# Eight plain steps and 32 doubles in a spectral layer with an MLP: plain steps that read the last 64 features from one tile, and a new plan for the work beside them

## The chip, the cores and the metric

The kernel runs on one core of one Trainium2 chip. A core has a matrix engine (TensorE, in the profile PE, with its weight loads as PEld), VectorE (DVE), ScalarE (ACT), GpSimd (POOL) and SyncE (SP), which issues nearly all DMAs. Each engine works off a queue of its own in order and waits on semaphores for the others. SBUF is the on-chip memory; TensorE writes to PSUM, from where VectorE and ScalarE fetch the results. The metric is device time in microseconds (us).

## The reference

```python
def layernorm(x): ...                                   # over the last axis
X = rfft2(layernorm(x)) * (w_r + 1j * w_i)              # x: 1 x 2048 x 576
h = x + irfft2(X, s=(2048, 576))
h2 = h + relu(layernorm(h) @ w1) @ w2                   # w1: 576 x 4608, w2: 4608 x 576
```

Everything is fp32. A matmul of the MLP is written as three products of rounded parts: each operand is split into a high part (`hi`) and the rest (`lo`), and hi·hi, hi·lo and lo·hi are added up in PSUM.

## The kernel before

**Forward stage** (0 to 31 us). The Fourier transforms are matmuls with fixed tables. The 2048 rows form 16 row tiles; for each tile t VectorE takes the statistics (`stat1`, `aggr1`, `row1`), GpSimd a power (`pow1`, L255), VectorE and GpSimd a sum and a difference (`add1` L263, `sub1` L258), ScalarE scales the table (`scale1`, L267, L268), and `fwd_a(t)` does eight matmuls of 64x128 and four of 64x64 (`rest`) for each half and lets ScalarE move the result out of PSUM. The steps of neighbouring tiles are interleaved by the loop over t.

**Middle and inverse stages** (to about 150 us). Sixteen frequency groups are multiplied by the weights and transformed back. The string `STEPS` sets the order by hand: each word is one call, and a word with "=" is a job that is told of below. `project(t)` (words j) writes the normalized rows, transposed, into the tile `xc[c]` of their chunk of 512 rows (c = 0 to 3): places 0 to 4 hold the hi part of the 576 features, 6 to 9 the lo part, and the 64 rows of the last 64 features stand in place 2. Behind the last `project` of a chunk five DMAs on SyncE (L579, L580), the "spread", copy these rows, 32 at a time, to other rows of places 5 and 2.

**Plain steps.** A step (g, c) applies weight group g (256 of the 4608 hidden features) to chunk c. `mm1(i, a)` makes one half of the hidden tile of step i: 14 matmuls of 128x512, the last two for the last 64 features, of which one reads place 2 and one place 5. When both halves are there, ScalarE takes the hi part out of PSUM (L638) and VectorE the lo part (L639). `mm2(i, q)`, q = 0 to 3, makes one output tile of 128 rows: 12 matmuls of 128x288, and VectorE adds the result to the output (L632). The list `steps` has ten steps, numbered from 0; END is the last. `mm1` of step i + 1 is written ahead of `mm2` of step i. From step 3 on one PSUM bank serves mm1 and three others rotate through mm2 (`ring`); the last output tile of step END − 1 is done in two halves.

**Doubles.** The other weight groups are done for two chunks at a time: `doubles` lists (g, p), and pair p = 0 means chunks 0 and 1, p = 1 chunks 2 and 3. A double is a scheme in the manner of Strassen and Winograd with seven products, each with 7 matmuls of 128x512 (`l1_prod`, L826) and 12 of 128x288 (`second`, L931), VectorE adding the results (L941). `slot(d)` interleaves the first halves of double d + 1 with the second halves of double d, and `slot_last` does the last one, half of it as plain products. `weights(d, r)` spreads the weight work for the next doubles over a slot.

**Work beside the plain steps.** Doubles need sums of the chunks' rows, T1 to T4. They are made in eight groups (0 to 7), each by these jobs: L loads a group (SyncE), S makes the four sums (two on VectorE, L673 and L674, two on GpSimd, L675 and L676), H and I take the hi parts (ScalarE), W and X the lo parts (VectorE, two pairs of L694 and L695 in a job). Results of pair 1, and some of pair 0, pass through buffers (`stage`) and are stored to memory from there, to be loaded again by `load_sum`. The first doubles' weights are summed on GpSimd (`w1_sums`, `w2_sums`) and split into hi (ScalarE) and lo (mostly GpSimd, some VectorE). The list `JOBS` says which job follows which `mm2`, from step 3 on. Queues run in the order in which this is written.

## Time and profile before

| | |
|---|---|
| time, median of 3 runs (lowest, highest) | 965.82 us (965.75, 966.11) |
| the profiled execution's own time | 965.46 us |
| its span | 963.7 us |
| granted TensorE clock, mean | 0.999 |
| first double's first product (L826) | at 258.10 us |
| last matmul of TensorE starts its last group | at 957.28 us |

The span runs from the first to the last instruction of the profile; some 1.8 us of the time lie outside it. A row of the timeline has the start, the length, the engine, the line, the operation, the written and read tiles by name, the shapes and the count. A row of a group has the busy time, the mean length of one in ns, and the idle time before its members with what ended it. TensorE's matmuls overlap in the records, so that the distance of two starts tells more than a length.

### The profile page before, as it was taken

The numbers are of one execution on the slowest core, as the hardware profiler recorded it, in microseconds if no ns is written. First come the engines' busy times: TensorE is split into PE (matmuls) and PEld (weight loads), VectorE is DVE, ScalarE is ACT, GpSimd is POOL, SyncE is SP. The second block draws the span as 40 slices with busy tenths as digits, with TensorE's granted clock in tenths as the row PEclk, the third lists the DMA queues.
The fourth block names the chain that finished last, engine by engine and source line by source line (L and its number), as shares of the span: only waits on it lengthen the run. The fifth ranks groups of instructions, "written<-read, shape, count | busy, mean of one in ns | idle before, by whom it ended". The sixth has DMA issues, their size and how long they took to land.

```text
span 963.7 us, 18094 instructions
## 1 busy us (share of the span) xinstructions
PE 955.7 (99%) x6658; PEld 850.1 (88%) x6658; DVE 770.6 (80%) x1226; ACT 466.7 (48%) x912; POOL 646.1 (67%) x783
## 2 busy tenths in 40 slices
PE   9999999999999999999999999999999999999997
PEld 7777778999988999999999999999999999999997
DVE  8577996687768888887888888888878888878886
ACT  6544558323355454545445444554554545444441
POOL 7213787514788777878686878767787768687842
PEclk9999999999999999999999999999999999999999
DMA  7974727557639264563728091836456372819365
GB/s 205 237 188 111 183 97 261 170 205 256 212 118 326 90 238 145 185 199 129 257 71 302 29 325 45 284 98 231 152 176 207 122 262 66 303 35 318 103 213 154
DMA packets 122840, 176.09 MB, mean 183 GB/s; under 512 B 7552, under 2 KB 102400, under 8 KB 122752
## 3 DMA queue, kind: packets, MB, share of 16 engines
q1 hardware_dynamic: 121584, 173.61, 55.9%
q10 hardware_dynamic: 1168, 1.33, 0.4%
q8 instruction: 53, 0.87, 0.4%
q14 instruction: 35, 0.29, 0.1%
HBM read 150.53 MB, written 23.07 MB: 180 GB/s over the span
## 4 chain that ended last, share of the span: by engine, by line
PE 96%; DVE 1%; DMA 1%; ACT 1%; issue 0%; SPq 0%; POOL 0%
PE h L826 36%; PE d L931 35%; PE d L156 24%; DMA C<-C 1%; PE d L564 1%; PE h L931 0%; DMA X<-in_A_x_dram 0%; DVE st L242 0%; ACT X L159 0%; ACT e L159 0%; ACT C L159 0%; DVE A L941 0%; DVE e L414 0%; DVE e L415 0%; DVE A L937 0%
## 5 line engine op out<-in xcount | busy, mean ns | idle before, releaser
L941 DVE TENSOR_TENSOR A<-A,d 128x576 f32<-128x576 f32 x428 | 317.5, 752 | 84.1 <-PE d L931 71.2
L931 PE MATMUL d<-X,D 128*128 128x288 f32 x1476 | 224.3, 294 | 0.1
L931 PEld LDWEIGHTS d<-X,D 128*128 128x128 f32 x1476 | 211.0, 188 | 10.5 <-DVE A L941 0.3
L826 PE MATMUL h<-B,e 128*128 128x512 f32 x658 | 166.8, 392 | 0.0
L159 ACT ACTIVATE e<-h 128x512 f32<-128x512 f32 x93 | 55.6, 597 | 188.0 <-PE h L826 187.9
L826 PEld LDWEIGHTS h<-B,e 128*128 128x128 f32 x658 | 118.3, 188 | 20.4
L353 POOL TENSOR_TENSOR e<-e,e 128x512 fp32r<-128x512 f32 (+3 forms) x68 | 89.8, 1320 | 57.9 <-ACT e L159 55.3
L642 ACT ACTIVATE e<-e 128x512 f32<-128x512 f32 x93 | 58.8, 633 | 107.5 <-DVE e L884 45.2
L826 PE MATMUL h<-X,e 128*128 128x512 f32 x434 | 110.0, 392 | 0.0
L353 POOL TENSOR_TENSOR X<-e,X 128x576 fp32r<-128x576 f32 (+1 forms) x34 | 49.9, 1469 | 62.8 <-ACT X L159 60.7
L826 PEld LDWEIGHTS h<-X,e 128*128 128x128 f32 x434 | 78.0, 188 | 13.4
L159 ACT ACTIVATE e<-e 128x256 fp32r<-128x256 f32 (+5 forms) x171 | 78.6, 489 | 14.3 <-DVE e L673 6.1
L850 POOL TENSOR_TENSOR A<-e 128x256 f32<-128x256 f32 x61 | 48.0, 787 | 28.4 <-DVE X L840 25.3
L840 DVE TENSOR_TENSOR D<-A,D 128x512 fp32r<-128x512 f32 x61 | 63.3, 1038 | 1.7 <-ACT D L159 1.7
L931 PEld LDWEIGHTS d<-X 128*128 128x128 f32 x372 | 55.6, 188 | 5.3 <-issue 0.4
L931 PE MATMUL d<-X 128*128 128x288 f32 x372 | 58.9, 294 | 0.1
L931 PE MATMUL d<-X,e 128*128 128x288 f32 x360 | 57.1, 294 | 0.0
L826 PE MATMUL h<-F,e 128*128 128x512 f32 x217 | 55.0, 392 | 0.0
L852 POOL TENSOR_TENSOR A<-e,A 128x256 f32<-128x256 f32 x61 | 52.9, 867 | 0.8 <-DVE A L848 0.8
L156 PE MATMUL d<-e,D 128*128 128x288 f32 x384 | 53.3, 295 | 0.0
L826 PE MATMUL h<-C,e 128*128 128x512 f32 x210 | 53.3, 393 | 0.0
L156 PEld LDWEIGHTS d<-e,D 128*128 128x128 f32 x384 | 51.9, 188 | 1.4 <-DVE A L632 0.4
(174 smaller groups left out, 1850.9 us busy)
## 6 DMA issues: line engine op xcount, KB each, us to landing
X<-t0T SPq DMA_DIRECT2D x16, 768.0 KB
X<-t1T SPq DMA_DIRECT2D x16, 768.0 KB
e<-in_B_w_dram SPq DMA_DIRECT2D x18, 576.0 KB
e<-in_B_w_dram SPq DMA_DIRECT2D x18, 512.0 KB
X<-t0T SPq DMA_DIRECT2D x16, 512.0 KB
X<-t1T SPq DMA_DIRECT2D x16, 512.0 KB
B<-t1T SPq DMA_DIRECT2D x8, 768.0 KB
B<-t1B SPq DMA_DIRECT2D x8, 768.0 KB
```

Of the source, the lines that this page charges most:

```text
L156: nc.tensor.matmul(o, l, r, start=start, stop=stop)
L159: nc.scalar.activation(o, i, AF.Copy, **kw)
L353: eng.tensor_sub(l, v, h)
L564: nc.tensor.transpose(pz[:, 128 * ORDER[b]:128 * ORDER[b] + 128], y[:, 128 * b:128 * b + 128], ident)
L642: nc.scalar.activation(o, i, AF.Relu)
L826: nc.tensor.matmul(o, a, b, start=bool(first) and n_ == 0, stop=n_ == len(ops) - 1, skip_group_check=not first)
L840: (eng or nc.vector).tensor_sub(f[1], v, f[0])
L850: nc.gpsimd.tensor_sub(s3, p0[:, :256], p0[:, 256:])
L852: nc.gpsimd.tensor_sub(s4, p1_[:, :256], s2)
L931: nc.tensor.matmul(P[tt], l[:, q], r, start=first and n_ == 0, stop=end and n_ == 2, skip_group_check=whole and not first)
L941: nc.vector.tensor_add(xt, xt, P)
```

## The change

The plain steps (2, 3) and (2, 2) go, and a double (2, 1) comes as the last one, so that the doubles are (2, 0), all pairs of groups 3 to 17, and (2, 1): 32 in place of 31. The weight work of `weights` runs on through the last slots, and the outputs of pair 0 are stored one slot earlier.

In the plain steps both matmuls of the last 64 features read place 2: the weight tile holds the 64 rows twice, in hi (`rest[0]`), and in lo with zeros below (`rest[1]`). So the spread is no longer read by plain steps. It becomes a job: F does the four DMAs to place 5, G the one within place 2. The small lo part of `project` is made on GpSimd (j) or VectorE (J), as the string says.

In the forward stage odd tiles do `rest` first and even tiles last, and the last tile's steps stand within the loop's own turn, its subtraction on VectorE.

`JOBS` has 31 entries, one at each place where `work()` is called: behind each `mm1` and `mm2` of steps 3 to 6, and in the seven turns of the last step. A "d" puts lows (W, X) or a weight split (V) on VectorE, otherwise they are on GpSimd; R runs a part of the weights' preparation, V a split, T a load. V4 is the split of T12, V5 that of T34. `stage` grows from four buffers to six.

```diff
+        elif t % 2:
+            rest(p)
         for h in range(2):
             for k in range(2):
                 for j in range(2):
                     q = slice(64 * j, 64 * j + 64)
                     mm(p[:, 512 * j + 128 * h:512 * j + 128 * h + 128], dims(G[q], (k, 321 - k)[h], [2, 128]),
                        caf[q, 64 * k:64 * k + 128], k == 0, k == 1)
-        if not end:
+        if t % 2 == 0:
             rest(p)
         act(dims(zx, 2 * t, [2048, 5 - end], [32, 64], [1, 2]), dims(p, 0, [64, 5 - end], [1, 64], [512, 2]))
 
...
             sub1(t)
         if t < NT:
             aggr1(t)
-        if old:
+        if 1 <= t < NT:
             scale1(t - 1)
+        if t == NT - 1:
+            row1(t)
+            pow1(t)
+            add1(t)
+            sub1(t, nc.vector)
+            scale1(t)
         if t >= 2:
             fwd_a(t - 2)
 
...
+        if g < FIRST:
+            for k in range(2):
+                nc.sync.dma_start(v4[64 * k:64 * k + 64], w1[512:576, f])
+            return
...
-        for k in range(2):
-            split_rest(rest[k], v4[:, k], nc.gpsimd)
+        act(rest[0], v4)
+        nc.gpsimd.tensor_sub(rest[1][:64], v4[:64], rest[0][:64])
+        nc.gpsimd.tensor_sub(rest[1][64:], rest[0][64:], rest[0][64:])
...
-        made[t // CH] += 1
-        (nc.gpsimd if t < 8 and made[t // CH] < CH else nc.vector).tensor_sub(dst[64:, 2, q], zt[64:, 256:384], dst[64:, 2, q])
-        if made[t // CH] == CH:
-            u = dst.bitcast(F32)
+        eng.tensor_sub(dst[64:, 2, q], zt[64:, 256:384], dst[64:, 2, q])
+
+    def spread(c, half):
+        u = xc[c].bitcast(F32)
+        if half:
             for a, b in ((0, 32), (32, 32), (64, 96), (96, 96)):
                 nc.sync.dma_start(u[a:a + 32, 5], u[b:b + 32, 2])
+        else:
             nc.sync.dma_start(u[32:64, 2], u[0:32, 2])
...
-    steps = [(0, 0), (0, 1), (0, 2), (1, 1), (0, 3), (1, 3), (1, 0), (1, 2), (2, 3), (2, 2)]
-    FIRST = 2
+    steps = [(0, 0), (0, 1), (0, 2), (1, 1), (0, 3), (1, 3), (1, 0), (1, 2)]
...
-        ops += [(rest[h][:, f], 3 * h + 2) for h in range(2)]
+        ops += [(rest[h][:, f], 2) for h in range(2)]
...
-        def low(k):
+        def low(k, eng):
             for n_ in (("T1", "T3"), ("T4", "T2"))[k]:
                 hi, lo, v = parts[n_]
-                nc.vector.tensor_sub(lo, v[:, :2], hi[:, :2])
-                nc.vector.tensor_sub(hi[64:96, 2], v[64:96, 2], hi[64:96, 2])
+                eng.tensor_sub(lo, v[:, :2], hi[:, :2])
+                eng.tensor_sub(hi[64:96, 2], v[64:96, 2], hi[64:96, 2])
                 if n_ in outs:
...
-    doubles = [(FIRST, 0)] + [(g, p) for g in range(FIRST + 1, NG) for p in ((1, 0) if g % 2 == FIRST % 2 else (0, 1))]
+    GS = [*range(FIRST, NG), FIRST]
+    doubles = [(g, p) for k, g in enumerate(GS) for p in ((k + 1) % 2, k % 2)][1:-1]
...
-        if g == NG - 1 and k in DONE:
+        if d in (LAST - 2, LAST) and k in DONE:
...
-        g = doubles[max(d, 0)][0]
+        at = (max(d, 0) + 1) // 2
         turn = (d + 1) % 2
         if not turn and r == 0 and d > 0:
-            w2_split("T34", nc.vector)
+            w2_split("T34", nc.gpsimd if d == LAST else nc.vector)
             w2_split("B22", nc.gpsimd)
-        if g == NG - 1:
-            return
+            if d == LAST:
...
-                split(*HF["Y"]["S12"], fx["p1"][LAST % 2], eng=nc.gpsimd)
+                split(*HF["Y"]["S12"], fx["p1"][LAST % 2], eng=nc.vector)
...
+            if m == 1:
+                weights(d, 0)
...
-        "s11 B1 B2 s8 s9 r8 e15 s12 =K0 n10 e14 s14 T n8 s13 B3 A10 =L0 j10 A11 j9 j11 j8 B10 s15 n12 =L1 B11 V0 "
-        "B12 B13 n14 =P0 j13 j12 A20 =S0 V1 A21 j14 A30 =S1 j15 =L2 =L3 A31 B20 =P1 B21 =H0 B22 =W0 =H1 B23 =W1 "
-        "=S2 "
+        "s11 B1 B2 s8 s9 r8 e15 s12 =F1 =K0 n10 e14 s14 T n8 s13 B3 A10 =L0 J10 A11 J9 J11 J8 B10 s15 n12 =L1 "
+        "B11 V0 B12 B13 n14 =P0 J13 J12 A20 =S0 V1 A21 J14 A30 =L2 J15 =P1 =S1 A31 =F3 =H0 B20 =H1 =L3 B21 B22 =S2 =L4 =W0d B23 "
...
-            for _ in range(2):
+        if k:
+            for _ in range(3 - k):
                 v = ebuf([128, 1280], F32R)
-                stage.extend((v[:, :640], v[:, 640:]))
+                stage[:0] = v[:, :640], v[:, 640:]
+        if k == 2:
+            FT.pop("C")
...
-        "L4 / H2 I0 I1 / W2 X0 X1 / S3 L5 I2 / X2 H3 I3 / W3 X3 K1 / S4 L6 / "
-        "H4 I4 / W4 X4 / S5 L7 / H5 I5 / W5 X5 / S6 / H6 I6 / W6 X6 / S7 / H7 I7 / W7 / X7"
...
+        "H2/W1d K1 W2//R0 I0 I2 I1 X0d X1//S3 L5/X2d I3 S4 H3/R1 R2/X3 H4 L6 P2 W3d I4 W4d S5 H5/L7/X4d I5 W5//X5/S6/S7 F0 R3//I6 R4 H6 V4 X6d T3 I7 X7d/G0 T2 V5d/W6d H7 R5 W7d/R6//V1 V0 V3//R7/V2 V6////F2 G2//"
...
+        elif k == 4:
+            vs["s"] = ebuf([128, EW])
+            w2_bufs()
+            w2_sums()
+        elif k == 5:
+            w1_sums(0)
+        elif k == 6:
+            w1_bufs()
+            vs["f"] = ebuf([128, EW])
+            vs["r"] = vs["s"][:, 1024:1280], vs["f"][:, 1024:1280]
+            w1_sums(1)
+        elif k == 7:
+            load_w1(FIRST + 1, vs[1], vs[4])
...
+    ring.insert(1, ring.pop())
...
-            TF.update(B22=khalf(1, 1), T2=khalf(3, 0), T3=khalf(3, 1))
         for q in range(4):
             if q < 2:
                 mm1(i + 1, q)
+                work()
             mm2(i, q)
-            if (i, q) == (3, 1):
-                TS = sb([128, 5, 512], "F", dt=F32R)
...
-            for n_, k in (("T2", (7, 1)), ("T3", (7, 2))):
-                if k == (i, q):
-                    load_sum(doubles[0][1], n_)
-            if (i, q) == (END - 2, 2):
-                vs["s"] = ebuf([128, EW])
-                w2_bufs()
-                w2_sums()
-            if (i, q) in ((END - 2, 3), (END - 1, 0)):
-                w2_split(("T34", "T12")[q == 3], nc.gpsimd)
-            if i == END - 1:
-                if q == 0:
-                    w1_sums(0)
-                if q == 1:
-                    w1_bufs()
-                    fb0 = ebuf([128, EW])
-                    vs["r"] = vs["s"][:, 1024:1280], fb0[:, 1024:1280]
-                    w1_sums(1)
-                if q:
-                    for n_ in (("A11",), ("S12",), ("S34", "A2"))[q - 1]:
-                        w1_split(n_, nc.vector if n_ == "A2" else nc.gpsimd)
-                if q == 1:
-                    w2_split("B22", nc.gpsimd)
+            work()
     for i in (END,):
-        load_w1(FIRST + 1, vs[1], vs[4])
+        fb0 = vs["f"]
         load_sum(0, "T1", True)
         first_banks.close()
         narrow = ctx.enter_context(tc.tile_pool(name="ph", bufs=1, space=PSUM))
...
+            work()
             weights(-1, r)
```

Three places of the order. TensorE, the last tiles of the forward stage (d_ the PSUM tile, e_ the tile's rows and its table); before:

```order
L156 MATMUL d_544<-e_474 128x128 x8
L156 MATMUL d_544<-e_474 64x64 x4
L156 MATMUL d_572<-e_502 128x128 x8
L156 MATMUL d_572<-e_502 64x64 x4
L156 MATMUL d_600<-e_530 128x128 x8
L156 MATMUL d_600<-e_530 64x64 x4
```

and now:

```order
L157 MATMUL d_544<-e_474 64x64 x4
L157 MATMUL d_544<-e_474 128x128 x8
L157 MATMUL d_572<-e_502 128x128 x8
L157 MATMUL d_572<-e_502 64x64 x4
L157 MATMUL d_606<-e_530 64x64 x4
L157 MATMUL d_606<-e_530 128x128 x8
```

Groups of one form now adjoin at the border of two tiles.

VectorE, the queue at the end of the step before the last (A_ the output and some sums, X_ and e_ weights and sums, D_ the hidden tile, d_ PSUM); before, the last two jobs of lows, W7 and X7, with output adds (128x576 from d_) between them:

```order
L639 SCALAR_TENSOR_TENSOR D_3029<-d_2526,D_3028 128x1024
L632 TENSOR_TENSOR A_1399<-A_1399,d_2529 128x576
L694 TENSOR_TENSOR e_2463<-A_1399,e_2463 128x256
L695 TENSOR_TENSOR e_2463<-A_1399,e_2463 32x128
L694 TENSOR_TENSOR e_2463<-A_1399,e_2463 128x256
L695 TENSOR_TENSOR e_2463<-A_1399,e_2463 32x128
L632 TENSOR_TENSOR A_1399<-A_1399,d_2527 128x576
L694 TENSOR_TENSOR e_2464<-e_2291,e_2464 128x256
L695 TENSOR_TENSOR e_2464<-e_2291,e_2464 32x128
L694 TENSOR_TENSOR e_2464<-e_2291,e_2464 128x256
L695 TENSOR_TENSOR e_2464<-e_2291,e_2464 32x128
L632 TENSOR_TENSOR A_1399<-A_1399,d_2528 128x576
```

and now, from add(5,3), the output add of the step before, over the T34 split, W6 and W7 to add(6,0) and the eviction behind it:

```order
L646 TENSOR_TENSOR A_1397<-A_1397,d_2511 128x576
L366 TENSOR_TENSOR X_2061<-e_2894,X_2061 128x2x288
L708 TENSOR_TENSOR e_2401<-e_2277,e_2401 128x256
L709 TENSOR_TENSOR e_2401<-e_2277,e_2401 32x128
L708 TENSOR_TENSOR e_2401<-e_2277,e_2401 128x256
L709 TENSOR_TENSOR e_2401<-e_2277,e_2401 32x128
L708 TENSOR_TENSOR e_2716<-A_1397,e_2716 128x256
L709 TENSOR_TENSOR e_2716<-A_1397,e_2716 32x128
L708 TENSOR_TENSOR e_2716<-A_1397,e_2716 128x256
L709 TENSOR_TENSOR e_2716<-A_1397,e_2716 32x128
L646 TENSOR_TENSOR A_1397<-A_1397,d_2512 128x576
L653 SCALAR_TENSOR_TENSOR D_2938<-d_2509,D_2937 128x1024
```

Where an add stood between two jobs of lows, they now follow each other, and add(6,0), the last row but one, stands behind both of them and the split.

ScalarE, the same place; before (e_2463 and e_2464 stage buffers, X_2070 the weights, D_ a hidden tile's hi):

```order
L159 ACTIVATE X_2070<-e_2776 128x4x288
L159 ACTIVATE e_2463<-A_1399 128x384 x2
L159 ACTIVATE e_2464<-e_2291 128x384 x2
L638 ACTIVATE D_3028<-d_2526 128x1024
L159 ACTIVATE X_2070<-e_3119 128x2x288 x2
L638 ACTIVATE D_3139<-d_2526 128x1024
```

and now, from I6 to the hi part of the last hidden tile (X_2061 the weights T12 and T34, e_2401, e_2402 and e_2716 stage buffers):

```order
L160 ACTIVATE e_2716<-e_2277 128x384
L160 ACTIVATE e_2716<-e_2276 128x384
L160 ACTIVATE e_2401<-e_2277 128x384 x2
L160 ACTIVATE X_2061<-e_2894 128x2x288
L160 ACTIVATE e_2402<-e_2276 128x384 x2
L160 ACTIVATE X_2061<-e_2894 128x2x288
L160 ACTIVATE e_2716<-A_1397 128x384 x2
L652 ACTIVATE D_2937<-d_2509 128x1024
```

The hi parts of T12 and T34, which stood together behind the last sums, now stand between those of the sums: that of T12 ahead of I7, that of T34 ahead of H7.

88 lines of the change are left out of this document (48 added, 40 removed).

## The prediction

> **What bounds the kernel now.** I read the page's shares first, then TensorE's timeline over the plain steps, then the chain of waits over the doubles.
>
> ```profile
> PE 955.7 (99%) x6658; PEld 850.1 (88%) x6658; DVE 770.6 (80%) x1226; ACT 466.7 (48%) x912; POOL 646.1 (67%) x783
> PE 96%; DVE 1%; DMA 1%; ACT 1%; issue 0%; SPq 0%; POOL 0%
> ```
>
> TensorE is busy for 99% of the span, and 96% of the chain that ends last is its own work. So the time is TensorE's work plus the few places where it waits. A change pays by taking matmuls out or by closing such a place, and costs by opening one. The other engines matter only where TensorE would stand for them.
>
> TensorE's timeline of two stretches with plain steps (start, length, matmuls):
>
> ```profile
> 160.87 6.98 PE L156 MATMUL d<-C,F 128*128 128x512 f32 x28
> 167.69 0.71 PE L564 MATMUL d<-ident,e 128*128 128x128 f32 x5
> ...
> 194.30 3.38 PE L156 MATMUL d<-X 128*128 128x512 f32 x14
> 197.53 1.74 PE L156 MATMUL d<-e,D 128*128 128x288 f32 x12
> 199.10 3.38 PE L156 MATMUL d<-X 128*128 128x512 f32 x14
> ...
> 245.34 3.38 PE L156 MATMUL d<-C,e 128*128 128x512 f32 x14
> ...
> 258.10 1.78 PE L826 MATMUL h<-B,e 128*128 128x512 f32 x7
> ```
>
> Matmuls overlap, so I take start to start. A hidden half (14 matmuls of 128x512) takes 197.53 − 194.30 = 3.23, an output tile (12 of 128x288) 199.10 − 197.53 = 1.57, and a whole plain step (two halves, four tiles) 258.10 − 245.34 = 12.76. The chain of waits in the first doubles (start, length):
>
> ```profile
> 302.24 1.60 PE h L826 x7
> 303.84 1.58 PE d L931 x12
> 305.42 1.62 PE h L826 x7
> 307.04 1.58 PE d L931 x12
> 308.62 1.60 PE h L826 x7
> ```
>
> Two products of a double take 308.62 − 302.24 = 6.38, so one takes 3.19. A double is seven: 22.33. Nothing stands between these rows: in both stretches TensorE runs without a gap.
>
> **The change, part by part.** I work against the profiled execution's own 965.46, of which the span is 963.7; the median of the runs shown, 965.82, is 0.36 above it.
>
> *Steps for a double.* Two plain steps go, 2 × 12.76 = 25.52; one double comes, 22.33. The sum is **−3.19**, all on TensorE, in stretches where it never waits. A plain step still has 14 matmuls to a half (two of the rest before and after), so it keeps its length. The last double, written half as plain products, keeps its form.
>
> *Forward tiles.* Every odd tile now does its 64x64 matmuls ahead of its 64x128 ones, so that forms change once in a tile, not twice. ScalarE's evictions and GpSimd's work in this stage:
>
> ```profile
> 16.41 0.75 ACT L159 ACTIVATE A<-d 128x640 f32<-128x640 f32 x1 [0.17 <-PE d L156]
> ...
> 17.85 0.76 ACT L159 ACTIVATE A<-d 128x640 f32<-128x640 f32 x1 [0.19 <-PE d L156]
> ...
> L258 POOL TENSOR_TENSOR e<-X 128x288 f32<-128x288 f32 x13 | 11.6, 891 | 0.0
> L255 POOL TENSOR_TENSOR r<-r,half 128x1 f32<-128x1 f32 x13 | 7.4, 570 | 0.0
> ```
>
> A tile takes 17.85 − 16.41 = 1.44, and ScalarE waits 0.17 of it for TensorE; so TensorE's length counts. But GpSimd has 0.89 + 0.57 = 1.46 of (partly overlapping) work for a tile and no idle time, so it can be little faster. No row shows a change of form alone: the ends are nothing (GpSimd holds the pace) and ScalarE's whole wait, 14 × 0.18 = 2.5. I take **−0.5**, near the lower end, as GpSimd's rows are the nearer limit; its subtraction for the last tile goes to VectorE, which only shortens the end of the stage.
>
> *Row spreading.* Plain steps read the last 64 features from one place, so they wait for no spread. What that wait was:
>
> ```profile
> PEld d L156 <- DMA C<-C: 0.5, 1, 0.5
> ```
>
> By the timeline, the 28 matmuls from 160.87 to 167.69 took 6.82, where two halves are 6.46: **−0.36** at most and at least nothing; I take the whole, since this wait's cause is gone and the matmuls behind it have no other. The 18 spreads that remain are read only by doubles, and are issued plain steps ahead of them; two rest-weight loads in place of three, and 64-row weight splits, come ahead of all plain steps and beside the inverse's matmuls: nothing, and at most the same 0.36 if one of them came late.
>
> *SyncE's queue.* The spreads of chunks 0 and 2, ten DMAs, now stand between the stores of sums and the loads of the first double's operands. The chain of waits, at the old place of the spread:
>
> ```profile
> 156.88 0.57 SPq L579
> ```
>
> At 0.57 an issue, five delay what stands behind them by 2.9. Those loads are issued most of a plain step (12.76) before the double reads them: nothing, at most +2.9, and I take nothing.
>
> *Sums, weights and lows in 5 steps' time instead of 7.* From the fourth plain step on, VectorE, GpSimd and ScalarE make the eight groups of sums and the first doubles' weights beside TensorE. That work hardly shrinks (8 output adds and two hidden evictions go with the two steps), but its cover does, by 25.5 us. By the order it is densest in the last two plain steps. I count from the start of the half mm1(6,1) as 0: TensorE could start mm1(7,0) at 7.95, mm1(7,1) at 12.75, mm2(6,3) at 15.98 + 2 × 1.57 = 19.1, and its second half at 19.9. Three PSUM banks rotate through mm2: the first half of mm2(6,3) needs the bank that add(6,0) empties, the second half that of add(6,1). VectorE's queue puts two groups' lows, a weight split and an eviction ahead of them. VectorE's rows, alone and beside a busy GpSimd:
>
> ```profile
> 195.81 0.43 DVE L694 TENSOR_TENSOR e<-e,e 128x256 fp32r<-128x256 f32 x1
> 196.25 0.28 DVE L695 TENSOR_TENSOR e<-e,e 32x128 fp32r<-32x128 f32 x1
> ...
> 203.58 1.22 DVE L639 SCALAR_TENSOR_TENSOR D<-d,D 128x1024 fp32r<-128x1024 f32 x1 [0.52 <-ACT D L638]
> 204.72 0.74 DVE L632 TENSOR_TENSOR A<-A,d 128x576 f32<-128x576 f32 x1
> ...
> 209.62 0.56 DVE L674 TENSOR_TENSOR e<-X,e 128x384 f32<-128x384 f32 x1
> ...
> 244.21 1.15 DVE L694 TENSOR_TENSOR e<-A,e 128x256 fp32r<-128x256 f32 x1
> 245.37 1.43 DVE L695 TENSOR_TENSOR e<-A,e 32x128 fp32r<-32x128 f32 x1
> 246.82 0.86 DVE L694 TENSOR_TENSOR e<-A,e 128x256 fp32r<-128x256 f32 x1
> 247.70 0.73 DVE L695 TENSOR_TENSOR e<-A,e 32x128 fp32r<-32x128 f32 x1
> ...
> 251.15 0.46 DVE L695 TENSOR_TENSOR e<-e,e 32x128 fp32r<-32x128 f32 x1
> ```
>
> And what the lows wait for (GpSimd's sums, ScalarE's highs):
>
> ```profile
> L779 POOL TENSOR_TENSOR e<-e 128x288 f32<-128x288 f32 x1 | 0.8, 811 | 0.0
> L676 POOL TENSOR_TENSOR e<-X,e 128x384 f32<-128x384 f32 x7 | 8.2, 1165 | 34.7 <-DVE e L674 13.2 <-ACT e L159 8.2 <-PE d L156 6.8
> L159 ACT ACTIVATE X<-e 128x576 fp32r<-128x576 f32 x2 | 1.4, 682 | 0.8 <-POOL e L782 0.8
> L159 ACT ACTIVATE e<-e 128x384 fp32r<-128x384 f32 x17 | 8.5, 519 | 12.3 <-DVE e L673 6.1 <-DMA t1T<-e 3.9 <-POOL e L676 2.3
> ```
>
> A job of lows, two pairs, is 2 × 0.71 = 1.42 alone. The path to add(6,0): mm1(6,1) ends at 3.23; its eviction was over 2.47 behind the end of the half in before (202.33 to 204.80), so at 5.7. S7's two on VectorE, 1.12: 6.8. Its last on GpSimd, 1.1: 7.9. Four w2 sums, 3.25: 11.2. ScalarE's high of the T12 weights, 0.68, and the two of I7, which stand behind it, 1.04: 12.9. Then VectorE alone: lows X7 1.42, an add 0.75, the T34 split 0.7 (as ScalarE's high of that shape), lows W6 and W7 2.84, add(6,0) 0.75: 19.4, against 19.1. Behind it stand the eviction of mm1(7) 1.22 and add(6,1) 0.75: 21.3, where the second half could start at 19.9. TensorE stands **+1.4**.
>
> The ends: nothing, if the w2 sums run ahead of S7's sums. With GpSimd busy throughout, the eight lows at 244.21 to 251.61 took 7.4, less the add among them (0.74) 6.6, where alone they are 2.84; at that price twelve lows are 9.9, not 4.26, and the split twice as long: 1.4 + 5.6 + 0.7 = +7.7. I take 1.4, the price alone: GpSimd's own queue here is broken up by splits that wait for ScalarE, and W6 and W7, two thirds of the lows, fall among these.
>
> *The end.* Weight work runs on through the last pair of doubles, and one split (Y's S12) goes from GpSimd to VectorE in the slot before the last. There TensorE already waits for an add:
>
> ```profile
> 945.04 0.80 PE d L931 x6
> 945.84 0.02 issue
> 945.86 0.77 DVE A L941
> 946.63 0.14 issue
> 946.77 1.82 PE d L931 x12
> ```
>
> The mean of that kind on VectorE is 1.04 (the page's line of L840, 128x512), partly into idle gaps: between nothing and +1.0; I take **+0.3**. GpSimd's T34 and B22 splits, new in the last slot, have several products of 3.19 before their results are read.
>
> ```profile
> L840 DVE TENSOR_TENSOR D<-A,D 128x512 fp32r<-128x512 f32 x61 | 63.3, 1038 | 1.7 <-ACT D L159 1.7
> ```
>
> Sum: −3.19 − 0.5 − 0.36 + 1.4 + 0.3 = −2.35; 965.46 − 2.35 = 963.1 for a profiled run, and **963.5** beside the median.
>
> **The rivals.** The measurement can tell about 0.2%, 1.9 us, from no change.
>
> *The dense place takes the gain back (no change).* If the two jobs nearest to GpSimd's sums pay the price beside it, the wait is 1.4 + 8 × (0.83 − 0.36) = 5.2, less what is hidden by the 1.2 of the eviction: about 4. Then −3.19 − 0.5 − 0.36 + 4 + 0.3 = +0.25: 966.1. For it: those very GpSimd instructions stood beside the dear rows in before. Against: in before none of this reached TensorE, and the cheap rows are the more frequent.
>
> *VectorE becomes the bound of the last plain step (slower).* All twelve lows pay that price: +7.7, in sum +3.95, 969.8. It is slower by over 0.2% from a wait of 5.7, which is when more than two thirds of these lows stand beside GpSimd. The dear rows speak for it: 1.15 and 1.43 where the same instructions alone took 0.43 and 0.28.
>
> The Trainium skill, page "SBUF — State Buffer", section "Who interferes with whom", has a rule for this: a VectorE instruction with both inputs in SBUF reads its second through a port that GpSimd also reads by, and one blocks the other for a whole instruction. By that rule the trace agrees, since the adds, with one input in PSUM, keep their 0.74 to 0.76 there and the lows don't; taken at its word for all twelve lows, it leads to this rival's time, not to mine.
>
> *Small edits give nothing (no change).* Forward and spread save nothing, the end costs 0.3: −3.19 + 1.4 + 0.3 = −1.5, 964.3. GpSimd's full row in the forward stage speaks for it.
>
> **How the numbers follow.** My forecast, a wait under 1.8 in the dense place, gets 0.50; the gain taken back 0.27; slower 0.15; the small edits without effect 0.08. So faster 0.50, same 0.35, slower 0.15. The range: downward no wait, and half of the forward stage's larger end, −3.19 − 1.25 − 0.36 = −4.8, 961.0; upward to 968.5, a wait of about 6.4, which leaves out the worst of the slower case.
>
> **What would show it.** Plain steps at 12.76 and products at 3.19 unchanged, 32 doubles: the first term. Evictions in the forward stage 1.40 apart or less: the second. No wait of PEld for a DMA within xc: the third. TensorE's gaps ahead of and within mm2(6,3), the lows' lengths and what GpSimd does beside them: the fourth; under 1.8 us in all I am right, over 4 a rival is. A gap in the last two doubles longer than 1.2 would be my fifth term missed. I am wrong altogether if TensorE waits elsewhere: for sums or weights landing late in the first double, which the DMA queue on SyncE could bring about.

## The result, and the profile after

The changed kernel takes **974.6 us** (median of 5 runs, 973.11 to 975.4), the kernel before beside it 965.82: a ratio of 1.009, with an interval of 1.0075 to 1.0105. It is slower by nearly 9 us, where 963.5 was forecast, and lies above the range of 961.0 to 968.5. The profiled execution of it took 973.11, with a span of 971.3, that is 7.6 more than the span of before; all rows of this section are of it.

The page's shares of the changed kernel, and the chain that ended last:

```profile
PE 954.4 (98%) x6639; PEld 849.0 (87%) x6639; DVE 777.0 (80%) x1219; ACT 475.4 (49%) x931; POOL 682.9 (70%) x831
PE 74%; POOL 2%; DVE 1%; DMA 1%; issue 1%; ACT 0%; SPq 0%; POOLq 0%; ACTq 0%; DVEq 0%
```

TensorE has 19 matmuls fewer on record and yet the span is longer. Its share of the last chain fell from 96% to 74%, but that fall is not a measure of waiting: the shares add up to 79% only, since the profile follows this chain back no further than 208.86 us. What counts is that from there to 241.19 the chain doesn't touch TensorE and runs over a store's DMA, ScalarE, GpSimd and VectorE. Where TensorE stood is seen in TensorE's timeline (start, length, matmuls; in brackets how long it stood and what ended that):

```profile
160.54 6.61 PE L157 MATMUL d<-C,F 128*128 128x512 f32 x28
166.99 0.71 PE L578 MATMUL d<-ident,e 128*128 128x128 f32 x5
...
193.61 3.38 PE L157 MATMUL d<-X,e 128*128 128x512 f32 x14
...
206.37 3.38 PE L157 MATMUL d<-B,e 128*128 128x512 f32 x14
211.21 1.82 PE L157 MATMUL d<-X,D 128*128 128x288 f32 x12 [1.46 <-DVE A L646]
...
220.80 3.38 PE L157 MATMUL d<-C,e 128*128 128x512 f32 x14
...
232.53 3.02 PE L157 MATMUL d<-X,D 128*128 128x288 f32 x12 [1.97 <-DVE A L646]
239.40 1.61 PE L157 MATMUL d<-X,D 128*128 128x288 f32 x6 [3.84 <-DVE A L646]
241.19 1.81 PE L157 MATMUL d<-X,D 128*128 128x288 f32 x6 [0.19 <-DVE A L646]
242.80 1.45 PE L841 MATMUL h<-B,e 128*128 128x512 f32 x5
```

The rows at 206.37 and 220.80 are the halves mm1(6,0) and mm1(7,0), that at 242.80 the first double's first product. A plain step without a wait is 12.76 (206.37 − 193.61). The next two are 14.43 and 22.00, **+1.67** and **+9.24**. Every wait in them ends with an output add (L646). The prediction's path had those ahead of and within mm2(6,3); it had none ahead of mm2(5,0) (1.46) and none ahead of mm2(6,2) (1.97).

The waits of the last step are 1.97 + 3.84 + 0.19 = 6.0. The other 3.2 are matmuls that run slower behind them: six of 128x288 take 241.19 → 242.80, 1.61, where six of an undisturbed tile take half of 1.57. The profile's windows (stretch, length, busy time and count of PE, PEld, DVE, ACT, POOL, then the granted clock, the DMA share and GB/s) show the clock meanwhile, and who is busy:

```profile
220.80:242.80 22.00, 16.00 (x79) 13.88 (x77) 20.79 (x27) 8.53 (x17) 19.50 (x23) 0.85 0.97 330
234.00:237.00 3.00, 1.55 (x7) 1.20 (x6) 2.86 (x6) 0.92 (x3) 2.92 (x7) 0.63 1.04 385
240.00:242.00 2.00, 1.81 (x8) 1.47 (x7) 2.00 (x4) 0.00 (x0) 1.77 (x4) 0.50 1.04 410
242.00:244.00 2.00, 2.00 (x10) 1.82 (x9) 0.62 (x2) 0.00 (x0) 0.69 (x1) 0.73 0.88 295
```

TensorE's granted clock falls to as low as 0.50 behind the waits. The Trainium skill, page "TensorE: Matmul & The Clock Gate", section "Part 1: The HAM clock gate", says that the clock follows how busy TensorE has lately been; the granted 0.50 here agrees. VectorE is busy in 20.79 of the 22.00 us of the step, GpSimd in 19.50. VectorE's queue in that step (L708 and L709 the lows, L366 the T34 split, L646 the adds):

```profile
224.08 0.89 DVE L708 TENSOR_TENSOR e<-e,e 128x256 fp32r<-128x256 f32 x1
224.98 0.80 DVE L709 TENSOR_TENSOR e<-e,e 32x128 fp32r<-32x128 f32 x1
...
227.74 0.83 DVE L708 TENSOR_TENSOR e<-e,e 128x256 fp32r<-128x256 f32 x1
228.58 1.43 DVE L709 TENSOR_TENSOR e<-e,e 32x128 fp32r<-32x128 f32 x1
...
231.73 0.75 DVE L646 TENSOR_TENSOR A<-A,d 128x576 f32<-128x576 f32 x1
232.40 0.75 DVE L366 TENSOR_TENSOR X<-e,X 128x576 fp32r<-128x576 f32 x1
233.07 0.42 DVE L708 TENSOR_TENSOR e<-e,e 128x256 fp32r<-128x256 f32 x1
...
237.31 1.24 DVE L709 TENSOR_TENSOR e<-A,e 32x128 fp32r<-32x128 f32 x1
238.59 0.76 DVE L646 TENSOR_TENSOR A<-A,d 128x576 f32<-128x576 f32 x1
```

From 224.08 to 239.35 there is no gap. The four pairs of X6 and X7 take 7.6 of it (to 231.7), those of W6 and W7 5.5 (233.07 to 238.55): 13.1 for eight pairs, 1.64 each, where a pair alone is 0.71. mm2(6,2) stands until the add at 231.73, mm2(6,3) until that at 238.59.

The parts of the +7.6, worked out from these rows and those of before:

| part | forecast | measured in the profiled run |
|---|---|---|
| two plain steps for a double | −3.19 | −3.19 |
| up to the half at 193.61 (before 194.30): forward, spread and others | −0.86 | −0.69 |
| the two dense steps | +1.4 | +10.91 |
| from the first product to the end, without the added double | +0.3 | +0.57 (728.5 − 705.6 − 22.33) |

The last line goes by span less first product: 971.3 − 242.80 and 963.7 − 258.10. So one term is off by 9.5, and all else within 0.3. In the second row that is partly luck, as is told further down: the forward stage gave none of its 0.5, and 0.33 came from the inverse. The median is a further 1.5 above the profiled run.

### The profile page after: what moved, and what is told of

Its sections match the earlier page's. It is cut to its first block, busy times and chain, and to the rows that moved or that the text cites. A ratio compares the mean times of both kernels' runs of the same rounds, so it can differ in the third digit from the quotient of the medians.

```text
span 971.3 us, 18133 instructions
## 1 busy us (share of the span) xinstructions
PE 954.4 (98%) x6639; PEld 849.0 (87%) x6639; DVE 777.0 (80%) x1219; ACT 475.4 (49%) x931; POOL 682.9 (70%) x831
## 4 chain that ended last, share of the span: by engine, by line
PE 74%; POOL 2%; DVE 1%; DMA 1%; issue 1%; ACT 0%; SPq 0%; POOLq 0%; ACTq 0%; DVEq 0%
PE h L841 37%; PE d L946 36%; PE d L157 1%; DMA t1T<-e 1%; PE h L946 0%; DVE A L956 0%; POOL X L366 0%; DVE e L709 0%; ACT e L160 0%; POOL e L708 0%; DVE A L646 0%; POOL e L763 0%; POOL A L689 0%; POOL e L764 0%; DVE D L366 0%
## 5 line engine op out<-in xcount | busy, mean ns | idle before, releaser
L956 DVE TENSOR_TENSOR A<-A,d 128x576 f32<-128x576 f32 x442 | 328.0, 752 | 88.1 <-PE d L946 74.8
L946 PE MATMUL d<-X,D 128*128 128x288 f32 x1524 | 231.6, 294 | 0.3 <-issue 0.2
L946 PEld LDWEIGHTS d<-X,D 128*128 128x128 f32 x1524 | 217.8, 188 | 11.2 <-issue 0.5
L841 PE MATMUL h<-B,e 128*128 128x512 f32 x672 | 170.5, 393 | 0.0
L366 POOL TENSOR_TENSOR e<-e,e 128x512 fp32r<-128x512 f32 (+2 forms) x72 | 93.2, 1294 | 48.5 <-ACT e L160 48.2
L841 PE MATMUL h<-X,e 128*128 128x512 f32 x448 | 113.6, 393 | 0.0
L366 POOL TENSOR_TENSOR X<-e,X 128x576 fp32r<-128x576 f32 (+1 forms) x36 | 53.2, 1477 | 67.1 <-ACT X L160 64.7
L841 PE MATMUL h<-C,e 128*128 128x512 f32 x224 | 56.8, 393 | 0.0
L946 PEld LDWEIGHTS d<-X,e 128*128 128x128 f32 x372 | 52.5, 188 | 0.2
L863 POOL TENSOR_TENSOR A<-A,e 128x256 f32<-128x256 f32 x62 | 49.0, 790 | 4.9
```

What stands on the lines that cost most here:

```text
L366: eng.tensor_sub(l, v, h)
L841: nc.tensor.matmul(o, a, b, start=bool(first) and n_ == 0, stop=n_ == len(ops) - 1, skip_group_check=not first)
L863: eng.tensor_sub(s2, s1, p0[:, :256])
L946: nc.tensor.matmul(P[tt], l[:, q], r, start=first and n_ == 0, stop=end and n_ == 2, skip_group_check=whole and not first)
L956: nc.vector.tensor_add(xt, xt, P)
```

## The experiments

I had four theories: **C**, VectorE's lows are slow because they stand beside a busy GpSimd; **G**, GpSimd's own queue is too long for these steps; **S**, the stores of the sums keep the stage buffers, so that hi parts and all behind them come late; **H**, of the rest of the median: a weight load collides with another transfer, since a wait that held the queue is gone. All rows and distances are of each kernel's one profiled run. To compare the kernels I take two distances. **Delay** is the first product's start less that of mm1(6,0), less 2 × 12.76, so that what happened before the dense steps drops out. **Rest** is the span less the first product's start, so that it shows what is given back later.

| kernel | mm1(6,0) | first product | delay | rest |
|---|---|---|---|---|
| before (its last two plain steps) | 232.58 | 258.10 | 0 | 727.9 (with one more double) |
| after | 206.37 | 242.80 | 10.91 | 728.5 |
| no_lows_67 | 206.33 | 235.76 | 3.91 | 730.8 |
| no_weight_sums | 209.76 | 243.11 | 7.83 | 728.9 |
| low5_dve | 208.03 | 244.12 | 10.57 | 728.8 |
| no_stores, no_stores_b | 227.02, 238.84 | 260.47, 272.20 | 7.93, 7.84 | 729.4, 729.5 |
| no_pair1, no_pair1_b | 217.33, 233.74 | 242.85, 259.26 | 0, 0 | 728.2, 728.1 |
| w2_late | 207.54 | 239.11 | 6.05 | 730.7 |
| w2_late_x4 | 207.29 | 238.09 | 5.28 | 730.9 |
| w2_late_x4_hold | 206.31 | 236.15 | 4.32 | 730.9 |
| after_hold | 205.94 | 242.44 | 10.98 | 728.0 |

### All jobs of groups 4 to 7 away: no_pair1 and no_pair1_b

```diff
+        if name in "LSHIWX" and k > 3:
+            return
```

Four stores, each of 128x2560 and so as large as all that is stored of one sum, stand in for those left out, in no_pair1 just ahead of the plain steps' loop, in no_pair1_b ahead of the first step of `STEPS`.

> The changed kernel without the sums of groups 4 to 7 altogether (loads, sums, hi, lo and stores; four large stores of other data stand in as a source for the later loads). If the whole loss stems from these jobs, every plain step takes 12.76 us and the time is that of the matmuls taken out: 965.8 - 3.2 - 0.7 + 0.5 (end) = 962.4, between 961.5 and 963.5. If another cause lies in the last plain steps (the weights' preparation on GpSimd alone), a wait of over 2 us stays there and the time is above 965.

> The changed kernel without the sums of groups 4 to 7 (loads, sums, hi, lo and stores), the four stand-in stores now issued ahead of the inverse stage, so that they are through before the plain steps. If the whole loss stems from these jobs, every plain step takes 12.76 us, the first double starts near 232, and the time is 961.5 to 963.5. If the weights' preparation on GpSimd is late by itself, a wait of over 2 us stays ahead of the first product and the time is above 965.

Measured: 972.91 (972.36 to 974.05, ratio 1.0072 [1.005, 1.0095]) and 989.14 (ratio 1.0239 [1.0221, 1.0258]). The totals say nothing on the theories, since the stand-in stores themselves delay earlier work, by 11 us and by about 27 (mm1(6,0) at 217.33 and 233.74, for 206.37). Less that, both come to about 962, an estimate from these rows that agrees with what was expected. The plain steps of no_pair1_b on TensorE do:

```profile
233.74 3.38 PE L157 MATMUL d<-B,e 128*128 128x512 f32 x14
...
246.50 3.38 PE L157 MATMUL d<-C,e 128*128 128x512 f32 x14
...
259.26 1.79 PE L841 MATMUL h<-B,e 128*128 128x512 f32 x7
```

They are 12.76 apart, and both delays are 0: without these jobs, but with all weight sums and splits, nothing is late. The whole +10.91 needs the jobs of groups 4 to 7.

### No lows of groups 6 and 7: no_lows_67

```diff
+                if 4 * p + j < 6:
-                eng.tensor_sub(lo, v[:, :2], hi[:, :2])
-                eng.tensor_sub(hi[64:96, 2], v[64:96, 2], hi[64:96, 2])
+                    eng.tensor_sub(lo, v[:, :2], hi[:, :2])
+                    eng.tensor_sub(hi[64:96, 2], v[64:96, 2], hi[64:96, 2])
```

> The changed kernel without the lo subtractions of groups 6 and 7 (the jobs W and X of these two; the stores stay): 16 VectorE instructions that took 13.1 us between 224.1 and 238.6 us. Theory C (the lows on VectorE beside a busy GpSimd set the end of the last plain steps): the wait of TensorE in mm2(6,2) and mm2(6,3), 9.2 us, falls below 2, the first product of the first double starts near 234 instead of 242.8, and the time near 966. Theory G (GpSimd's queue of lows, sums and weight splits is the bound, up to the A11 split that ended at 240.5): the first product starts no earlier than 239, and the time stays above 970.

Measured: 968.53 (968.12 to 973.06), ratio 1.0039 [1.0018, 1.0059]. The delay falls by 7.0, to 3.9, and TensorE shows at once what is late next:

```profile
234.86 1.06 PE L157 MATMUL d<-X,D 128*128 128x288 f32 x6 [1.55 <-DVE A L646]
235.76 0.62 PE L842 MATMUL h<-B,e 128*128 128x512 f32 x2
237.69 2.50 PE L842 MATMUL h<-B,e 128*128 128x512 f32 x5 [1.31 <-POOL e L366]
```

The first product now stands in its middle for a weight split on GpSimd, which is the end of a queue that does not stand still from 228.16 to 240.3:

```profile
234.75 1.29 POOL L366 TENSOR_TENSOR e<-e,e 128x512 fp32r<-128x512 f32 x1
...
236.91 0.72 POOL L366 TENSOR_TENSOR e<-e,e 128x256 fp32r<-128x256 f32 x1
```

So without these lows most of the delay goes, and behind them stands GpSimd: of the 7.0, the rest of the program gives 2.3 back (730.8 for 728.5). Of the 3.9 that stay, 2.1 arise in the step before (mm1(7,0) at 221.18). The run leaves out the lows altogether, and so can't tell lows that are dear from lows that are there at all; the next one can.

### GpSimd without the weight sums: no_weight_sums

Every w1 and w2 sum on GpSimd is a memset of the same tile in place of the sums; the lows stay.

```diff
-            w2_sums()
+            nc.gpsimd.memset(vs["s"], 0.5)
...
-            w1_sums(0)
+            nc.gpsimd.memset(vs["s"][:, :1024], 0.5)
```

> The changed kernel with GpSimd's w2 and w1 sums in the plain steps (12 instructions of 0.46 to 0.85 us with inputs in SBUF, some 8 us) replaced by memsets, which read nothing. The lows on VectorE are all there. Theory C by the price beside GpSimd: with GpSimd's readers gone, the eight pairs of groups 6 and 7 fall from 1.64 us a pair towards the 0.71 of a pair alone (sum 13.1 to about 7), and the first product starts 5 to 7 us earlier. Rival (the lows are late, not dear): the pairs keep 1.4 or more, and the first product moves only by what GpSimd's chain does.

Measured: 972.77 (971.8 to 973.75), ratio 1.0072 [1.0053, 1.009]. The total hardly moves. In the profiled run the dense steps began 3.4 later (209.76), all of it lost ahead of the plain steps, where a weight load came late (the last experiment is about that). The delay falls by 3.1, and VectorE's queue shows the lows themselves:

```profile
229.05 0.43 DVE L708 TENSOR_TENSOR e<-e,e 128x256 fp32r<-128x256 f32 x1
229.49 0.28 DVE L709 TENSOR_TENSOR e<-e,e 32x128 fp32r<-32x128 f32 x1
...
236.76 1.38 DVE L708 TENSOR_TENSOR e<-A,e 128x256 fp32r<-128x256 f32 x1
238.17 0.69 DVE L709 TENSOR_TENSOR e<-A,e 32x128 fp32r<-32x128 f32 x1
```

The same eight pairs take 8.6 (a stand of 1.00 between them left out) in place of 13.1, and where GpSimd works again (the splits, from 236.7 on) one is 2.1. The lows are the same instructions on the same data sizes, so their price is set by what GpSimd does, and it isn't GpSimd's being busy that does it: the two rows at 229.05 and 229.49 began while a memset of 1.17 ran (from 228.39 on). **C is shown for the price**. For the delay it is a part: 3.1 went, where 5 to 7 were expected. mm2(6,3) still stands 3.78 here, behind a hi part that came 1.00 late, the last pair's 2.1 and a clock of 0.50. The Trainium skill, page "SBUF — State Buffer", section "Who interferes with whom", adds to the rule in the prediction that a GpSimd instruction which only writes SBUF does not block VectorE's second input, and this agrees: 0.71 a pair beside memsets, 1.64 on the mean beside sums and splits.

### The lows of group 5 moved from GpSimd to VectorE: low5_dve

```diff
-        "... L7/X4d I5 W5//X5/ ..."
+        "... L7/X4d I5 W5d//X5d/ ..."
```

> The changed kernel with the lows of group 5 (W5, X5) on VectorE instead of GpSimd. Theory G: GpSimd's queue is four pairs shorter (about 5 us), everything behind it 3 to 4 us earlier, and the time falls to about 971. Theory C: VectorE has 2.8 us (alone) to 6.6 us (beside GpSimd) more ahead of add(6,0), and the time rises by 0 to 4, to 975 to 978.

Measured: 974.1 (973.46 to 974.74), ratio 1.0083 [1.0054, 1.0113]: the same as after, with a delay of 10.57 for 10.91. What GpSimd is relieved of in the step before, VectorE pays. G got no support here, but it wasn't refuted either: GpSimd then stood 5.12 for VectorE ahead of one of its sums (at 221.91), so that its w2 sums began 2.8 behind mm1(7,0), for 3.8 in after.

### No stores of the sums: no_stores and no_stores_b

```diff
-                if n_ in outs:
-                    keep(p, n_, (640 * j, outs[n_]))
```

Six stand-in stores replace them, at the two places told of above.

> The changed kernel without the stores of the sums (six large stores of other data ahead of the fourth plain step stand in, so that the later loads have a source): the hi parts no longer wait for a stage buffer to be written out. Theory S (ScalarE's hi parts wait 4 to 5 us for stores that land 5.6 us after their issue, and pass the delay on through the queues of ScalarE, GpSimd and VectorE): the wait of 1.6 us ahead of mm2(5,0) goes, GpSimd's lows of group 5 start 3 to 4 us earlier, and the time falls by 4 to 6, to about 969. Theory C: the lows stay beside GpSimd's weight work, and the time falls by less than 2.

> The changed kernel without the stores of the sums, the six stand-in stores now issued ahead of the inverse stage. Theory S (hi parts wait for stores to land and pass it on through three queues): the wait of 1.6 us ahead of mm2(5,0) goes, GpSimd's lows of group 5 start 3 to 4 us earlier, the first product starts 4 to 6 us earlier than 242.8, and the time falls to 968 to 970. Theory C (lows beside GpSimd's weight work): the lows keep their price, and the time falls by no more than the 1.6, to 973. The loads of other groups may also land sooner, which this run does not tell from S.

Measured: 992.02 (ratio 1.0269) and 1003.38 (ratio 1.0387); again the stand-ins spoil the totals, in no_stores_b by some 32 us ahead of mm1(6,0). In both the delay is 7.8 to 7.9, so 3.0 of the 10.9 hang on the stores, 0.8 of it in the step before and the rest in the last (no_stores_b). There the eight pairs still take 12.5, for 13.1 (the wait within the last step is 4.96 long); they only begin earlier, 1.5 behind mm1(7,0) for 3.3. What the stores do is seen in ScalarE's row of after in the step before, ahead of mm2(5,0): four hi parts wait until a store has emptied their buffers, VectorE's lows of W4 wait for these, and the add behind them ends the 1.46:

```profile
207.13 1.77 ACT L160 ACTIVATE e<-e 128x384 fp32r<-128x384 f32 x4 [4.27 <-DMA t0T<-e]
```

Without stores the wait ahead of mm2(5,0) is 0.68 (no_stores_b) and 0.83. **S is a quarter of it**, not the whole; loads that land sooner with the stores gone may be in that quarter, which these runs don't tell apart.

### The w2 sums and their splits put off: w2_late, and X4 later: w2_late_x4

The w2 sums, which run on GpSimd beside the lows of X6 and X7, move behind the last plain step's first products, with the splits V4 and V5; A11, the split that no_lows_67 waited for, goes first.

```diff
-        "... I6 R4 H6 V4 X6d T3 I7 X7d/G0 T2 V5d/ ... /V1 V0 V3//R7/V2 V6////F2 G2//"
+        "... I6 R4 H6 X6d T3 I7 X7d/G0 T2/ ... /V0 V1 V3//R7/V2 V6/R8 V4 V5d///F2 G2//"
```

w2_late_x4 has, besides, X4's lows one place later, behind the third output add of the step in place of the second. It was meant to free the add for which mm2(5,0) waits. But that is add(4,1), since three banks rotate, and in VectorE's queue it stands ahead of X4's lows in either kernel; what stands ahead of it are W4's, which the edit leaves in place:

```diff
-        "... /L7/X4d I5 W5//X5/ ..."
+        "... /L7//X4d I5 W5/X5/ ..."
```

> The changed kernel with the four w2 sums and the splits of T12 and T34, which only the first double's second halves read, put off into the last step (behind the S34 split), and the A11 split ahead of the S12 split. Theory G (GpSimd's queue up to the A11 split is the bound): 4.9 us of sums and split and 2.0 of the S12 split go from ahead of A11, the first product starts 5 to 7 us earlier, and the time falls to 968 to 970. Theory C: VectorE loses only the T34 split (0.75) and stands beside GpSimd's w1 sums as before; the first product starts 1 to 2 us earlier, and the time falls to 973. If the put-off work is too late for the first double, a new wait shows at its L946 matmuls near 262.

> The kernel with the late w2 sums, and the lows X4 (with I5 and W5) one place later, behind the output adds that TensorE waited for ahead of mm2(5,0). If the order of VectorE's queue makes that wait (the adds stand behind lows whose hi part waits for a store), it falls from 1.7 or more to under 0.5, and the time to 970 to 971. If the stores only move the wait on, the jobs of group 5 come later by as much, and the time stays at 972 to 974.

Measured: 972.33 (971.6 to 973.06), ratio 1.0065 [1.0047, 1.0084], and 970.76 (970.66 to 970.85), ratio 1.0051 [1.0032, 1.0069]. In w2_late three of the eight pairs (227.29 to 229.52) are back at their own price:

```profile
227.29 0.43 DVE L708 TENSOR_TENSOR e<-e,e 128x256 fp32r<-128x256 f32 x1
227.73 0.28 DVE L709 TENSOR_TENSOR e<-e,e 32x128 fp32r<-32x128 f32 x1
```

GpSimd stands idle beside them, as its own row shows:

```profile
230.50 0.74 POOL L763 TENSOR_TENSOR e<-e 128x256 f32<-128x256 f32 x1 [3.81 <-DMA e<-in_B_w_dram]
```

The delay falls by 4.9, to 6.05, between what theory C had expected (1 to 2) and theory G (5 to 7). The edit takes work both from GpSimd's queue and from beside the lows, so it doesn't part the two. Of the 4.9, 2.2 come back in the first double, as TensorE's rows of w2_late show, one wait for an operand's load and one for the very split that was put off:

```profile
243.29 1.65 PE L841 MATMUL h<-X,e 128*128 128x512 f32 x6 [0.60 <-DMA X<-t0T]
...
260.96 0.92 PE L946 MATMUL d<-X 128*128 128x288 f32 x5 [1.53 <-POOL X L366]
```

w2_late_x4 takes another 0.8 off the delay, but not by its order. The wait that it was to bring under 0.5 is still there:

```profile
212.99 1.81 PE L157 MATMUL d<-X,D 128*128 128x288 f32 x12 [2.32 <-DVE A L646]
```

In w2_late it is 2.69. The step from mm1(6,0) to mm1(7,0) takes 17.2 there and 15.3 here: 0.4 of the difference is wait, and 1.6 is clock, since behind the wait it was 0.65 in w2_late, for 2.4 us, and 1.00 here. The last step is 1.2 longer here. So the 0.8 is what is left of a clock that happened to stay whole in one profiled run, and that X4's place helps isn't shown; the intervals of the two ratios overlap. The waits in its last step (222.57 to 238.09) are 1.50 and 0.74, and the window around that step reads 1.00:

```profile
220.80:242.00 21.20, 18.64 (x111) 16.39 (x109) 16.87 (x28) 9.03 (x19) 15.33 (x20) 1.00 0.98 328
```

So half of the delay went in these runs, and near half of that returned: the work has to be done somewhere before the first double ends.

### The small edits on the kernel before: before_place2_fwd, before_place2_b

The kernel before with place 2 for both matmuls of the rest, and in _fwd the forward stage's new order too.

```diff
+        if g < 2:
+            for k in range(2):
+                nc.sync.dma_start(v4[64 * k:64 * k + 64], w1[512:576, f])
+            return
...
-        ops += [(rest[h][:, f], 3 * h + 2) for h in range(2)]
+        ops += [(rest[h][:, f], 2 if g < 2 else 3 * h + 2) for h in range(2)]
```

> The kernel before with two parts of the change alone: plain steps of groups 0 and 1 read the last 64 features from place 2, and odd tiles of the forward stage do their 64x64 matmuls first (the last tile's steps stay where they were). My prediction's second and third term: 0.5 and 0.36 faster, 965.0. If the forward stage is held by GpSimd, as in the changed kernel's trace, only 0.36: 965.45. Rival: the stretch behind the spread is waited for elsewhere and both are worth nothing: 965.8.

Measured: 967.26 (966.37 to 967.52), ratio 1.001 [1.0001, 1.0019]. The forward stage gained nothing: its evictions stood at 0.1 to 0.2 behind those of before near 29 us. The run doesn't test the spread: one DMA of it, the one within place 2, was still issued ahead of the matmuls, which waited 0.80 for it and then read rows that it had replaced. before_place2_b has no change in the forward stage and issues that DMA only behind the plain steps that read the place, as the changed kernel does.

> The kernel before with one part of the change: plain steps of groups 0 and 1 read the last 64 features from place 2, and the DMA within place 2 comes only in the later plain steps (the forward stage is as before). My third term: the 28 matmuls behind the spread take 6.46 instead of 6.82, and the time is 965.45. If the hi part in place 2 is itself late there, 965.8.

Measured: 966.63, ratio 1.0009 [1.0, 1.0018], but with runs from 965.15 to 970.18, where those of before beside it lie within 1.3 us. Its profiled run, 968.12, shows a wait that no theory had. Of before, from the timelines of GpSimd, SyncE's queue (L481 is the reload of x) and ScalarE (the hi part of a 128x1152 tile of w2):

```profile
84.78 0.52 POOL L339 MEMSET G<- 128x512 f32 x1
...
85.33 1.27 SPq L335 DMA_DIRECT2D G<-in_B_w_dram  x3
...
88.29 7.78 SPq L481 DMA_DIRECT2D A<-in_A_x_dram  x10
...
91.87 1.16 ACT L159 ACTIVATE e<-e 128x1152 fp32r<-128x1152 f32 x1 [0.84 <-DMA e<-in_B_w_dram]
```

and of before_place2_b, SyncE's queue, ScalarE and TensorE:

```profile
86.19 9.30 SPq L490 DMA_DIRECT2D A<-in_A_x_dram  x8
94.96 1.16 ACT L159 ACTIVATE e<-e 128x1152 fp32r<-128x1152 f32 x1 [3.27 <-DMA e<-in_B_w_dram]
...
100.61 1.45 PE L156 MATMUL d<-X,cc 64*64 64x288 f32 x14 [1.80 <-issue]
```

In before, a GpSimd memset of the tile G, done at 85.30, held SyncE's queue ahead of a rest-weight load until 85.33; place 2 needs no zeros there, so memset and hold are gone, x is reloaded from 86.19 on (88.29 in before), beside the load of w2, and w2 lands 3.1 later, although its load was issued earlier (85.63, in before 86.70).

### The hold put back: before_place2_hold, after_hold, w2_late_x4_hold

```diff
-    load_weights(0, sb([128, 512], "G")[:, :256])
+    hold = sb([128, 512], "G")
+    nc.gpsimd.memset(hold, 0.0)
+    load_weights(0, hold[:, :256])
```

> The kernel before with the last 64 features read from place 2, as in the run before, but with GpSimd's memset of the tile G kept ahead of the first rest-weight load, where the kernel before has it. In before, SyncE stood 1.6 us for that memset, and the loads of x behind it started later. Theory H (without that stop the loads of x start 2.7 us earlier, run beside the load of the w2 weights, and make it land after 92.4 us, when ScalarE's queue and then TensorE stand for it): the spread of the times falls back to that of before (1.3 us or less), and the median to 965.3 to 965.6, as the spread's wait of 0.36 is gone. Rival (the load of w2 varies by itself, or the 64-row loads make it late): the times still reach 967 to 970, with a median above 966.2.

> The changed kernel with the same memset kept ahead of the first rest-weight load. Theory H: its times (973.1 to 975.4) shrink to within 1 us, and the median falls to about 973. Rival: the spread stays at 2 us and the median at 974.6.

> The changed kernel with the three edits that helped: late w2 sums with A11 first, X4 one place later, and the memset kept. Theory H with the earlier results added up: 970.8 less the 0.8 that its profiled run lost near 98 us, 970.0. If waits of one stage hide behind those of the next, as between the late w2 sums and the stores, it gains less, 970.5.

Measured: 965.68 (965.39 to 966.99), ratio 1.0 [0.9991, 1.0009]; 972.94 (972.23 to 973.36), ratio 1.0074 [1.0059, 1.009]; 970.67 (968.81 to 971.06), ratio 1.0045 [1.0032, 1.0059]. In after_hold the reload of x is late again, and w2 early:

```profile
87.75 8.32 SPq L497 DMA_DIRECT2D A<-in_A_x_dram  x11
91.42 1.16 ACT L160 ACTIVATE e<-e 128x1152 fp32r<-128x1152 f32 x1 [0.69 <-DMA e<-in_B_w_dram]
```

The same row, w2's hi part, shows the collision over all profiled runs: it begins between 91.42 and 91.96 in the four kernels with the hold, and between 91.43 and 94.96 in the twelve without, in two of these no later than with it. So the collision is shown, and it comes in some runs only.

Its price is not. after_hold's median is 1.7 under that of after, and the runs spread over 1.1 in place of 2.3, but the intervals of the two ratios overlap. For place 2 on the kernel before, the median falls by 1.0 and the spread from 5.0 to 1.6, as wide as that of before beside it; but before_place2_fwd, without the hold, spread over 1.2 only. On w2_late_x4 the hold gained 0.1 (970.67 for 970.76), where 0.3 to 0.8 were expected, and its four runs spread over 2.3. So I put the price at 0 to 1.7 us. w2_late_x4 and the hold together stay 4.7 above before.

In before_place2_hold the place of the old spread, on TensorE:

```profile
161.46 6.62 PE L156 MATMUL d<-C,F 128*128 128x512 f32 x28
167.91 0.71 PE L575 MATMUL d<-ident,e 128*128 128x128 f32 x5
```

The two halves take 6.45, not 6.82: the spread's term is there, and too small for the total to show.

## Why the prediction was wrong

**The first term, −3.19, was right.** Undisturbed plain steps kept 12.76, and the products of the doubles their 3.19.

**The forward stage, −0.5, gave nothing.** The last eviction began at 30.77, in before at 30.73. GpSimd's row, on which the lower end rested, mostly keeps its 1.34 us for a tile in both kernels, so it is the likely bound; no run tested that, and in the changed kernel GpSimd also stood 1.5 for VectorE. Another 0.3 was gained in the inverse, in the matmuls between 123 and 126 us; its cause is open, and it is luck that it nearly fills the place of the 0.5.

**The spread, −0.36, was right** (160.54 to 166.99 is 6.45), and so was the end: the wait ahead of the last groups grew by 0.37 (953.07 to 954.54, in before 945.67 to 946.77), behind the split that VectorE took over. The rest of the +0.57 is mostly a gap of 0.25 in the first double.

**The step that failed is the fourth, "Sums, weights and lows in 5 steps' time instead of 7".** Its place was right and its mechanism was named, but I chose the low end: "I take 1.4, the price alone: GpSimd's own queue here is broken up by splits that wait for ScalarE". In the trace that queue is hardly broken up where it matters: GpSimd worked 19.50 of 22.00 us. The twelve lows of X7, W6 and W7, for which I had 4.26, took 3.96 + 5.48 = 9.44; the slower rival had 9.9. By that rival the wait was +7.7; against my count from mm1(6,1) (212.87), mm2(6,3) could start at 239.40 − 212.87 = 26.5 and not at 19.1, 7.4 late. So the case to which I gave 0.15 is the one that came, and no_weight_sums shows why the lows were dear: GpSimd's reads beside them.

**The loss was more than that rival's, by four things that I did not count**, three in this term and one outside it.
- X6's lows: I had them done ahead of ScalarE's high at 12.9, that is at 225.8; beside GpSimd they took until 227.7. Of the 7.4 above they are 1.9, the twelve lows 5.2, and 0.3 was in the forecast.
- The granted clock: behind the waits it fell to 0.50 to 0.73, and with it, and a last wait of 0.19, the 7.4 at mm2(6,3) grew to 9.24 at the first product.
- The step before: +1.67, by a wait ahead of mm2(5,0), where I had looked for none; its add stands behind lows whose hi part waits for a store, and it is 0.68 with the stores gone.
- A removed hold, H: 0 to 1.7 of the median, at a place that I had put at nothing, and at most 0.36. I had asked what SyncE's added DMAs delay, not what SyncE's removed wait had kept apart.

**What lies behind.** The lows alone are not the whole delay (no_lows_67 leaves 3.9 of it), nor are the stores (3.0 less) or weight sums (3.1 to 4.9 less); each alone takes off a part, the parts overlap, and what is late next is GpSimd's queue. The same work had two plain steps more as cover in before. Whether some order makes eight plain steps pay stays open: none of those here came below before, and moving the last two groups' hi parts and lows into the last plain step, behind mm2(6,3)'s adds, wasn't tried.

## What to carry to other kernels

When steps are taken out of a stage that TensorE bounds, the work beside it loses their cover: add up what each helping engine has left to do there, at the price that its instructions have beside the other busy engines, and if two of them come near the length of the stage, the dear rows are the ones to count with. Look at every wait ahead of an add that frees a PSUM bank, not only at the last. A wait on a DMA queue that an edit removes may have kept two transfers apart.

## What was not expected of the hardware

- A wait of some microseconds can cost more than itself: 6.0 us of waits in the last plain step brought 3.2 more by a clock of 0.50 to 0.73. Its length alone doesn't settle that. Behind the same 1.83 at the same place, one kernel's next 12 matmuls took 2.57 from start to start, at a clock of 0.60, and the other's 1.66, at 1.00; in w2_late_x4 a wait of 2.32 left the clock at 1.00, too. after_hold, then no_weight_sums:

```profile
211.16 2.78 PE L157 MATMUL d<-X,D 128*128 128x288 f32 x12 [1.83 <-DVE A L648]
...
214.97 1.82 PE L157 MATMUL d<-X,D 128*128 128x288 f32 x12 [1.83 <-DVE A L646]
```

- The small low (32x128) can pay more than the large: 0.28 alone, 1.43 beside a GpSimd subtraction of 1.62 that began 0.33 before it:

```profile
228.25 1.62 POOL L366 TENSOR_TENSOR X<-e,X 128x576 fp32r<-128x576 f32 x1
```

- Large stores disturb far ahead of where they matter: the six stand-in stores of no_stores_b, issued ahead of the first step of `STEPS`, moved mm1(6,0) from 206.37 to 238.84.
